# Splitting the memory copies of 41 segments into column halves, reordering the last scratch loads, and a new instruction order

## The chip, the cores and the metric

One core of a Trainium2 chip runs the whole program in a single launch. The metric is device time in microseconds (us), the median of three runs. Engine names are those of the profile: PE is TensorE (PEld its weight loads), DVE is VectorE, ACT is ScalarE, POOL is GpSimd, SP is the sync engine that issues most transfers.

## The reference

Two kinds of block alternate, A, B, A, B, each added to its own input `x` of 2048 tokens by 512 features. Block A is attention over 64 segments of 32 tokens with 8 memory rows in front, and the memory rows of a segment's output are the memory of the next segment:

```python
mem = mem0
for s in range(n_seg):                       # 64 segments, one after the other
    h = concatenate([mem, xs], axis=1)       # 8 memory rows + 32 tokens
    q, k, v = h @ Wq, h @ Wk, h @ Wv         # 512 -> 32 heads x 128
    p = softmax(where(mask, q @ k.T * scale, -1e9))
    o = (p @ v) @ Wo                         # 32 heads x 128 -> 512
    mem = o[:, :M, :]                        # carried to the next segment
    outs.append(o[:, M:, :])
```

Block B is linear attention over all tokens with `phi(t) = where(t > 0, t + 1, exp(t)) + 1e-6`; its sums over the sequence must be complete before its first output row:

```python
kv = sum over tokens of phi(k) outer v;  z = sum over tokens of phi(k)
o = (phi(q) @ kv) / (phi(q) @ z + 1e-6)
return o @ wo
```

So 128 segments (64 in each of two A blocks) form one serial chain through the memory rows, and the program's end is a block B that has to wait for the last segment.

## The kernel before

The code records operations (nodes) with the engines that may run them, what they read and write and the PSUM bank they use; nothing runs when they are recorded. Two tables written out by hand then decide the order. `PLACE` gives every node, under the key (layer, step, name) and its running number, a place in the order and, where two engines could do it, the letter of the engine (`a` ACT, `v` DVE); `BANKS` gives each PSUM tile one of eight banks. `schedule` sorts all nodes by the table and `finalize` turns dependences between engines into semaphore waits. Each engine runs its own list strictly in order, so a node that waits holds back everything behind it on that engine.

A segment is a step `s`. The names in `PLACE` that matter here:

- `kq0`, `kq1`, `v`: the projections of a segment's 40 rows by Wk, Wq and Wv (`project`). The contraction of 512 is done in four chunks `c` of 128, and `hT` holds the rows transposed, chunk by chunk. `kq0` does K and Q together, for each chunk four matmuls of Wk and four of Wq that share the stationary rows.
- `mem0`, `mem1`: scores, softmax and values of the memory queries, the part the next segment waits for.
- `out`: the output projection by Wo (`out_proj`), 64 matmuls of 256 columns into one PSUM tile. One copy then moves the tile (128 partitions x 256) to `outW`. Column halves 0:128 and 128:256 of `outW` hold what becomes chunks 0 and 2, and chunks 1 and 3, of the next segment's memory columns.
- `next` (`next_mem`): small matmuls with a selection matrix `selm`, four per half, transpose and add the memory rows into a PSUM tile of 32 columns; one copy writes them into the memory columns of `hT`. `kq0` of the next segment waits for that copy.
- `x`: the attention of the 32 tokens, which nothing waits for at once. It and the projections of other blocks (`left`, `bi`, `lq`, `bo`) fill PE while the chain above waits.

At the end, block B of the second layer (`last_rows`, `last_queries`, `b_out`) reads its inputs back from scratch memory in HBM, into the room of the A weights. SP loads, each after the one before it: `pt_scratch` (ready queries) into Wq's room, `xn_scratch` (normalized rows, whose queries are still to be computed) into Wk's room, and `xs_scratch` (the residual rows). `LATE[1]` names the eight row tiles 4 to 11 whose queries `last_queries` computes at the end, as PE work `lq` from `XN(4)` and `XN(8)`:

```python
for w, (vw, nm, free, t0) in enumerate(((pt_view, "pt", [], 3.4), (xs_view, "xs", rows, 3.4))):
    for i in range(0, NT - 1, 4):
        ...
        if prev is not None:
            nd.order.add(prev)
```

For i = 4 and 8 the first pass loads `xn_scratch`, for i = 0 and 12 `pt_scratch`. The load into Wk's room waits for the last matmul that reads Wk.

Of the kernel before, what the change touches and what calls it, by code (L numbers as in the profile page):

```python
# [1626 lines left out]
def c_dve(n, rate=1):  # L1627
    return 0.155 + 1.044e-3 * n / rate
# [246 lines left out]
def _build_kernel(nc, A_x, A_mem0, A_Wq, A_Wk, A_Wv, A_Wo, A_seg_len, B_wqkv, B_wo, out):  # L1875
# [3 lines left out]
    DH = A_Wq.shape[2]  # L1879
# [3 lines left out]
    NT = S // 128  # L1883
# [1184 lines left out]
```

## Time and profile before

| what | value |
|---|---|
| time, three runs | 1455.92, 1456.2, 1457.59 us; median 1456.2 |
| profiled execution | 1458.68 us, of which the span of the instructions is 1456.7 us |
| PE busy | 1432.7 us, 98% of the span, 43649 matmuls |
| DVE, ACT, POOL busy | 1241.8 (85%), 903.4 (62%), 202.5 us (14%) |
| mean granted TensorE clock | 0.999 |

PE's row says how much time is left to win: 1456.7 less 1432.7 is 24.0 us in which no matmul was under way. Matmuls overlap and their ends are modelled, so a wait of PE that is shorter than the last matmul's tail doesn't show as idle time; the weight-load queue's waits (PEld) show such short ones.

### The profile page before, as it was taken

To read this page: it belongs to the slowest core of one execution; us is meant where nothing else is said; L and a number is where in the kernel's file an instruction comes from. 1 tells how busy PE (TensorE), PEld (TensorE's weight loads), DVE (VectorE), ACT (ScalarE), POOL (GpSimd) and SP (SyncE) were. 2 spreads that over 40 slices of the span, in tenths; PEclk is the share of its full clock that TensorE was granted. 3 is DMA by queue.
4 is the path that set the end of the run, shared out by engine and by line. 5 is a ranking of instruction groups with operands and counts; after the bars stand their busy time and mean duration, and the time that the engine had idled before them with its cause. 6 is when DMAs were issued, how large, how long until landed. Compare 5 with 4: busy or idle time off the path is not lost.

```text
span 1456.7 us, 90916 instructions
## 1 busy us (share of the span) xinstructions
PE 1432.7 (98%) x43649; PEld 834.5 (57%) x39545; DVE 1241.8 (85%) x3910; ACT 903.4 (62%) x2588; POOL 202.5 (14%) x407
## 2 busy tenths in 40 slices
PE   9999999999999999999999999999999999999988
PEld 4555555555565656555465555565656655556555
DVE  6879888898888888888888888888888888888878
ACT  4456656556655666656656666666666666665547
POOL 3111111111111110111101111011101011111100
PEclk9999999999999999999999999999999999999999
DMA  9422112111110010101201111111101011110133
GB/s 384 177 60 39 33 28 47 25 25 25 23 25 22 14 26 24 26 25 49 75 16 22 36 32 26 28 29 36 25 18 25 26 28 29 25 26 21 35 76 128
DMA packets 79255, 66.96 MB, mean 46 GB/s; under 512 B 55480, under 2 KB 70648, under 8 KB 77336
## 3 DMA queue, kind: packets, MB, share of 16 engines
q1 hardware_dynamic: 64872, 42.04, 10.7%
q0 software_dynamic: 13840, 18.98, 4.5%
q8 instruction: 325, 5.32, 1.6%
q14 instruction: 58, 0.48, 0.1%
q10 hardware_dynamic: 160, 0.14, 0.0%
HBM read 31.33 MB, written 14.94 MB: 32 GB/s over the span
## 4 chain that ended last, share of the span: by engine, by line
PE 95%; DVE 2%; DMA 1%; ACT 1%; issue 1%; SPq 0%
PE pb L2283 44%; PE pb L2564 20%; PE pb L2140 15%; PE pb L2152 3%; PE pb L2514 3%; PE pb L2757 2%; PE pb L2472 2%; PE pb L2534 2%; PE pb L2436 2%; PE pb L2594 1%; DMA Wk_sb<-in_A_Wk_dram 1%; PE pb L2444 1%; DMA Wk_sb<-xn_scratch 1%; ACT arena_sb L2009 0%; DVE arena_sb L2489 0%
## 5 line engine op out<-in xcount | busy, mean ns | idle before, releaser
L2009 ACT ACTIVATE arena_sb<-pb 128x512 bf16<-128x512 f32 (+3 forms) x993 | 491.0, 524 | 240.6 <-PE pb L2140 112.0
L2283 PE MATMUL pb<-Wk_sb,arena_sb 128*32 128x512 bf16 x4320 | 358.7, 380 | 2.1 <-DVE arena_sb L2010 0.9
L2564 PE MATMUL pb<-Wo_sb,arena_sb 128*32 128x256 bf16 x10368 | 326.5, 273 | 1.4 <-issue 0.7
L2283 PE MATMUL pb<-Wv_sb,arena_sb 128*32 128x512 bf16 x4608 | 327.6, 378 | 0.0
L2564 PEld LDWEIGHTS pb<-Wo_sb,arena_sb 128*32 128x32 bf16 x10368 | 265.0, 97 | 43.9 <-DVE arena_sb L2479 12.9
L2302 DVE STREAM_TRANSPOSE arena_sb<-arena_sb 128x256 f32<-128x256 f32 x640 | 259.2, 426 | 27.1 <-ACT arena_sb L2009 20.1
L2027 POOL DMA_DIRECT2D dx_sb<-y_sb x246 | 125.0, 512 | 908.8 <-DVE y_sb L2576 398.0
L2283 PE MATMUL pb<-Wq_sb,arena_sb 128*32 128x512 bf16 x3088 | 234.4, 379 | 0.6 <-issue 0.6
L2283 PEld LDWEIGHTS pb<-Wk_sb,arena_sb 128*32 128x32 bf16 x4320 | 118.8, 96 | 177.6 <-issue 89.1
L2487 ACT ACTIVATE arena_sb<-pb,arena_sb 128x128 bf16<-128x128 f32 x538 | 163.8, 369 | 65.9 <-DVE arena_sb L2521 25.7
L2140 PE MATMUL pb<-Wq_sb,arena_sb 128*32 128x512 bf16 x2032 | 200.9, 379 | 0.0
L2010 DVE CAST arena_sb<-pb 128x512 bf16<-128x512 f32 (+2 forms) x274 | 141.9, 521 | 51.0 <-PE pb L2140 19.9
L2489 DVE TENSOR_TENSOR arena_sb<-pb,arena_sb 128x128 bf16<-128x128 f32 (+2 forms) x391 | 157.4, 403 | 8.6
L2009 ACT ACTIVATE outW_sb<-pb 128x256 f32<-128x256 f32 (+1 forms) x142 | 54.3, 383 | 174.5 <-PE pb L2564 124.4
L2283 PEld LDWEIGHTS pb<-Wv_sb,arena_sb 128*32 128x32 bf16 x4608 | 113.8, 95 | 70.6 <-issue 6.6
L2283 PEld LDWEIGHTS pb<-Wq_sb,arena_sb 128*32 128x32 bf16 x3088 | 85.1, 97 | 88.0 <-issue 25.2
L2514 PE MATMUL pb<-arena_sb 128*32 128x130 bf16 x3072 | 105.7, 219 | 1.1 <-issue 1.1
L2502 DVE TENSOR_TENSOR arena_sb<-arena_sb,wx_sb 128x1280 bf16<-128x1280 bf16 x128 | 102.2, 799 | 1.9 <-ACT arena_sb L2455 1.4
L2524 DVE STREAM_TRANSPOSE arena_sb<-arena_sb 128x192 f32<-128x192 f32 x256 | 93.4, 365 | 10.7 <-ACT arena_sb L2487 7.7
L2576 DVE TENSOR_TENSOR y_sb<-pb,outW_sb 64x256 bf16<-64x256 f32 x162 | 68.8, 424 | 19.8 <-ACT outW_sb L2009 15.3
L2514 PEld LDWEIGHTS pb<-arena_sb 128*32 128x32 bf16 x3072 | 67.3, 96 | 29.8 <-issue 8.5
L2472 PEld LDWEIGHTS pb<-arena_sb 128*32 128x32 bf16 x2016 | 47.3, 95 | 63.9 <-ACT arena_sb L2009 31.3
(135 smaller groups left out, 1819.1 us busy)
## 6 DMA issues: line engine op xcount, KB each, us to landing
Wk_sb<-in_A_Wk_dram SPq DMA_DIRECT2D x4, 1024.0 KB, 9.8
Wq_sb<-in_A_Wq_dram SPq DMA_DIRECT2D x4, 1024.0 KB, 17.7
Wv_sb<-in_A_Wv_dram SPq DMA_DIRECT2D x4, 1024.0 KB, 25.5
Wo_sb<-in_A_Wo_dram SPq DMA_DIRECT2D x8, 512.0 KB, 22.2
xs_scratch<-x_sb POOLq DMA_DIRECT2D x32, 128.0 KB, 2.0
pq_scratch<-arena_sb POOLq DMA_DIRECT2D x23, 128.0 KB, 2.1
xn_scratch<-arena_sb POOLq DMA_DIRECT2D x20, 128.0 KB, 2.9
lk_scratch<-arena_sb POOLq DMA_DIRECT2D x8, 256.0 KB, 3.5
```

The source lines that it names most:

```text
L2009: return e.activation(o() if callable(o) else o, i() if callable(i) else i, ACTF.Copy)
L2010: return e.tensor_copy(o() if callable(o) else o, i() if callable(i) else i)
L2027: add(eng, lambda e: e.dma_start(o, i), 0.55 if eng == "pool" else 0.66, reads=reads, writes=writes, dsem="%s%d" % (kind, k), lat=lat + (0 ...
L2140: return pe.add_instruction(mybir.InstMatmult(name=nc.get_next_instruction_name(), engine=mybir.EngineType.PE, ins=[pe.lower_ap(x), pe.low ...
L2283: r = pe.matmul(o, blk[:, c, :], w, start=(c == 0), stop=(c == 3), tile_position=(0, 32 * j))
L2302: add("dve", lambda v: v.transpose(dst, src(img[:, k, :].bitcast(F32))), 0.445, reads=[("img", k, h) for h in range(2)], writes=[dkey])
L2487: x = e.activation(o[:, u, :], i()[:, u, :], ACTF.Copy, scale=r[:, u:u + 1])
L2489: return e.tensor_tensor(o, i(), r.unsqueeze(2).to_broadcast([128, n, 128]), ALU.mult)
L2502: add("dve", lambda v: v.tensor_tensor(Px.rearrange("p b (n j x) -> p b n j x", n=20, j=4), PQx[:, r2].rearrange("p b (n x) -> p b n x", n ...
L2514: r = pe.matmul(pv.f32()[32 * i:32 * i + 32, 130 * k:130 * k + 130], cols(b, k, i), vimg[:, r2, 4 * b + i, :], start=True, stop=True, skip ...
L2524: add("dve", lambda v, b=b, k0=k0: v.transpose(oTb[:, s1, b, :, :, k0:k0 + 3].rearrange("p h j k q e -> p k (h j) (q e)").bitcast(F32), ox ...
L2564: r = pe.matmul(tl.f32()[32 * j:32 * j + 32, 0:256], oT[:, b, f, n, :, :, e], Wo_sb[:, 16 * b + 4 * n + 2 * f + e, 256 * d:256 * d + 256], ...
```

## The change

Three things are changed, and then everything is ordered anew.

1. `halved(s)` is true for steps 0 to 27 and 58 to 62 of the first layer and 0 to 2 and 58 to 62 of the second: 41 segments. In these the copy to `outW` is recorded as two copies of 128 columns; each half of `next` goes to a PSUM tile of its own and has its own copy, of 16 columns; and `kq0` of the segment that follows takes the chunks in the order 0, 2, 1, 3, of which 0 and 2 wait for the copy of half 0 and 1 and 3 for that of half 1.
2. The loads at the end go in the order i = 4, 8, 0, 12 in both passes: `xn_scratch` ahead of `pt_scratch`, and of the residual rows tiles 4 and 8 ahead of 0 and 12.
3. `PLACE` and `BANKS` are replaced as a whole.

```diff
+        def halved(s):
+            return (layer == 0 and (s < 28 or 57 < s < 63)) or (layer == 1 and (s < 3 or 57 < s < 63))
...
-            for c in range(4):
+            cs = (0, 2, 1, 3) if own else (0, 1, 2, 3)
+            for n, c in enumerate(cs):
...
-                add("pe", mm, 0.2155 * len(parts), reads=sorted({p[1] for p in parts}) + sorted({(p[1], 0, c) for p in parts}) + bkeys, tiles=tls)
+                add("pe", mm, 0.2155 * len(parts), reads=sorted({p[1] for p in parts}) + sorted({(p[1], 0, c) for p in parts}) + bkeys + (own[c % 2:c % 2 + 1] if own else []), tiles=tls)
...
-            nd = evac(outW[cc, v, :], lambda: tl.f32()[cc, 0:256], 256, tiles=[tl], writes=[("outW", w)])
-            nd.quad = (0, 0) if urgent else (2, 2)
+            c0 = P.count
+            for h in ((0, 1), (1, 2)) if urgent and halved(int(P.place[1])) else ((0, 2),):
+                if h[1] - h[0] < 2:
+                    P.count = 21 + h[0]
+                o = slice(128 * h[0], 128 * h[1])
+                evac(outW[cc, v, o], lambda o=o: tl.f32()[cc, o], 128 * (h[1] - h[0]), tiles=[tl], writes=[("outW", w, i) for i in range(*h)])
...
-                add("pe", mm, 0.06, reads=[("outW", w), "selm"], tiles=[tl])
+                add("pe", mm, 0.06, reads=[("outW", w, h), "selm"], tiles=[tls[h * apart]])
...
+            for h in range(2):
+                P.count = 11 + h
+                evac(dst[:, h], lambda h=h: tls[h].f32()[:, 16 * h:16 * h + 16].rearrange("p (d m) -> p d m", d=2), 16, tiles=[tls[h]],
+                     writes=[("hTm", G1 % 2, g1, h)])
...
-                    tk, tq = project(blk, bk, *parts)
+                    tk, tq = project(blk, bk[:1], *parts, own=bm) if s and halved(s - 1) else project(blk, bk, *parts)
...
-            for i in range(0, NT - 1, 4):
+            for i in (4, 8, 0, 12):
...
-    (0, 5, "next"): "96577 96655 96996v",
+    (0, 5, "next"): "95860 96108 0 0 0 0 0 0 0 0 0 96200a 96697v",
```

Where the tables put things is seen in the engines' lists. First PE, from the output projection of segment 5 of the first layer (`Wo_sb` x64) to the projections of segment 6 (`Wk_sb`, `Wq_sb`); `selm_sb,outW_sb` is `next`, 32x130 is token attention. Before:

```order
L2564 MATMUL pb<-Wo_sb,arena_sb 32x256 x64
L2514 MATMUL pb<-arena_sb 32x130 x24
L2534 MATMUL pb<-arena_sb 32x130 x8
L2594 MATMUL pb<-selm_sb,outW_sb 32x16 x8
L2283 MATMUL pb<-Wv_sb,arena_sb 32x512 x4
L2140 MATMUL pb<-Wv_sb,arena_sb 32x512 x4
L2283 MATMUL pb<-Wk_sb,arena_sb 32x512 x4
```

And now:

```order
L2569 MATMUL pb<-Wo_sb,arena_sb 32x256 x64
L2288 MATMUL pb<-Wv_sb,arena_sb 32x512 x4
L2140 MATMUL pb<-Wv_sb,arena_sb 32x512 x4
L2605 MATMUL pb<-selm_sb,outW_sb 32x16 x4
L2519 MATMUL pb<-arena_sb 32x130 x12
L2605 MATMUL pb<-selm_sb,outW_sb 32x16 x4
L2519 MATMUL pb<-arena_sb 32x130 x12
L2288 MATMUL pb<-Wk_sb,arena_sb 32x512 x4
```

The eight small matmuls of `next` stand apart as four and four, and the filling work around them has changed sides: the left block's Wv projection went ahead of `next`, the token attention behind it.

On ACT and DVE one copy to `outW` has become two, and one copy of `next` two; in 36 of the 41 segments both halves of the output copy stand one right after the other on ACT.

SP near the program's end, with the loads into the rooms of Wq and Wk. Before:

```order
L2027 DMA dx_sb<-y_sb 24x256 x2
L2933 DMA Wq_sb<-pt_scratch 128x4x512
L2925 DMA Wk_sb<-xn_scratch 128x4x512 x2
L2027 DMA dx_sb<-y_sb 24x256
L2181 DMA_TRANSPOSE arena_sb<-pq_scratch 128x4x128
L2027 DMA pt_scratch<-arena_sb 128x512
L2933 DMA Wq_sb<-pt_scratch 128x3x512
L2932 DMA Wq_sb<-xs_scratch 128x4x512 x3
L2932 DMA Wq_sb<-xs_scratch 128x3x512
```

And now:

```order
L2027 DMA dx_sb<-y_sb 24x256 x2
L2943 DMA Wk_sb<-xn_scratch 128x4x512 x2
L2181 DMA_TRANSPOSE arena_sb<-pq_scratch 128x4x128
L2027 DMA dx_sb<-y_sb 24x256
L2951 DMA Wq_sb<-pt_scratch 128x4x512
L2027 DMA pt_scratch<-arena_sb 128x512
L2951 DMA Wq_sb<-pt_scratch 128x3x512
L2950 DMA Wq_sb<-xs_scratch 128x4x512 x3
L2950 DMA Wq_sb<-xs_scratch 128x3x512
```

The first load of ready queries went behind the two loads of rows, a transpose and a small move.

PE at the same end, from the last matmuls that read Wk as a weight to the first that compute queries from the loaded rows (`Wk_sb,arena_sb` under L2152). Before:

```order
L2283 MATMUL pb<-Wk_sb,arena_sb 32x512 x4
L2283 MATMUL pb<-Wv_sb,arena_sb 32x512 x4
L2564 MATMUL pb<-Wo_sb,arena_sb 32x256 x48
...
L2283 MATMUL pb<-Wv_sb,arena_sb 32x512 x24
L2564 MATMUL pb<-Wo_sb,arena_sb 32x256 x8
L2514 MATMUL pb<-arena_sb 32x130 x12
L2564 MATMUL pb<-Wo_sb,arena_sb 32x256 x16
L2514 MATMUL pb<-arena_sb 32x130 x12
L2534 MATMUL pb<-arena_sb 32x130 x16
L2564 MATMUL pb<-Wo_sb,arena_sb 32x256 x40
L2152 MATMUL pb<-Wk_sb,arena_sb 32x512 x16
```

And now:

```order
L2288 MATMUL pb<-Wk_sb,arena_sb 32x512 x16
L2569 MATMUL pb<-Wo_sb,arena_sb 32x256 x8
L2288 MATMUL pb<-Wq_sb,arena_sb 32x512 x8
L2288 MATMUL pb<-Wv_sb,arena_sb 32x512 x8
L2288 MATMUL pb<-Wq_sb,arena_sb 32x512 x8
L2569 MATMUL pb<-Wo_sb,arena_sb 32x256 x16
...
L2569 MATMUL pb<-Wo_sb,arena_sb 32x256 x40
...
L2288 MATMUL pb<-Wv_sb,arena_sb 32x512 x24
L2569 MATMUL pb<-Wo_sb,arena_sb 32x256 x8
L2519 MATMUL pb<-arena_sb 32x130 x12
L2539 MATMUL pb<-arena_sb 32x130 x8
L2152 MATMUL pb<-Wk_sb,arena_sb 32x512 x8
```

Left out in both are the scores' small matmuls, and before also 4 of Wv. Between the last use of Wk and the first use of the loaded rows there stood 32 matmuls by Wv, 112 by Wo and 40 of 130 columns; now there stand 32 by Wv, 16 by Wq, 72 by Wo and 20 of 130 columns.

More of the change, by code (lines that the diff above doesn't have):

```diff
@@ new lines @@
+    "6251745023450346220532345024026251353560426305243205340605273146743670671437630437304637704564035645"
+    "4171024103654127504374073076074245563436635217462764422521406624154752024060504757714605120465341062"
+    "3451274317362417337627436274716235714736146236561014471036540132710327074203154623724505607423754235"
+    "3042735405074372071560075436072153647534601731543672037210102473204703406516360532502365201460503465"
+    "2103570245246730264571025015213524713716505742034012543561435214305701556312304027107026130752043623"
@@ new lines @@
+    "2464676754024736042363512647325667106431006521716430567707236102734027746027703245561406541265164751"
+    "0745700461570515754602167242427366254702432410377023012150321604245366424236253524700536143204623471"
+    "2173551274513243461253070614763647516520135621256026013101442357601740510152731603612062560203476445"
+    "1674205747560247301524125725031641725637452472540075260471671363613063010751276414726047604261054741"
+    "0146441075216506130536340537065072560523720723607730760451670516041567300740411536207457250714105724"
@@ new lines @@
+    "0572475012632361437652746516274412564752652113624260452163571270275174205352407015047510707145165475"
+    "7011537366132327041534540560314357761060714363571423605370213174021357647056014462651357310463104135"
+    "0410627561732061756737664230751067407365073623072102041535144720647216020261367504235640635240205013"
+    "1647520767274062754267755742164513305476260744241565731246071524136020367205612345713741527305724317"
+    "1625065461310774330272036440157243167540301563126750432675456732560451466405320127170512360344320465"
@@ L1604 @@
+    "0626536245335312476507360473137562035165203452740760274506120115072167135053740231420142061275302725"
+    "6307211561546530120744376423241736070474072321054140760746276025307406310234510651067435275067142647"
+    "1627415076647420734033613205717250672046527014751204653015721072746503214571032470157463276327463263"
+    "1275467236325140150306452473541060070574417727643303025272221"
 )
@@ L2260, in at, with project, mm @@
             P.at(layer, s, name)
-        def project(blk, bkeys, *parts, fresh=0):
+        def halved(s):
+            return (layer == 0 and (s < 28 or 57 < s < 63)) or (layer == 1 and (s < 3 or 57 < s < 63))
+        def project(blk, bkeys, *parts, fresh=0, own=None):
             tls = [P.tile() for _ in parts]
-            for c in range(4):
-                def mm(pe, c=c):
+            cs = (0, 2, 1, 3) if own else (0, 1, 2, 3)
+            for n, c in enumerate(cs):
+                def mm(pe, c=c, n=n):
+                    first, last = n == 0, n == 3
                     for i, (tl, (W, key, b, across, *lo)) in enumerate(zip(tls, parts)):
@@ L2277, in mm @@
                             else:
-                                n = (8 * j + 4 * b) * DH
-                                w = W[:, c, n + lo:n + hi]
+                                at_ = (8 * j + 4 * b) * DH
+                                w = W[:, c, at_ + lo:at_ + hi]
                             if i and 4 * c + j >= fresh:
-                                r = again(pe, o, blk[:, c, :], w, c == 0, c == 3, (0, 32 * j))
+                                r = again(pe, o, blk[:, c, :], w, first, last, (0, 32 * j))
                             else:
-                                r = pe.matmul(o, blk[:, c, :], w, start=(c == 0), stop=(c == 3), tile_position=(0, 32 * j))
+                                r = pe.matmul(o, blk[:, c, :], w, start=first, stop=last, tile_position=(0, 32 * j))
                     return r
-                add("pe", mm, 0.2155 * len(parts), reads=sorted({p[1] for p in parts}) + sorted({(p[1], 0, c) for p in parts}) + bkeys, tiles=tls)
+                add("pe", mm, 0.2155 * len(parts), reads=sorted({p[1] for p in parts}) + sorted({(p[1], 0, c) for p in parts}) + bkeys + (own[c % 2:c % 2 + 1] if own else []), tiles=tls)
             return tls
@@ L2588, in next_mem, with mm @@
             G1, g1 = divmod(s + 1, 4)
-            tl = P.tile()
+            apart = halved(s)
+            tls = [P.tile() for _ in range(1 + apart)]
             for h in range(2):
-                def mm(pe, h=h):
+                def mm(pe, h=h, tl=tls[h * apart]):
                     for j in range(4):
@@ L2596, in mm @@
                     return r
-                add("pe", mm, 0.06, reads=[("outW", w), "selm"], tiles=[tl])
-            evac(hT[:, G1 % 2, g1, :, 0:8].rearrange("p (d h) m -> p h d m", d=2),
-                 lambda: tl.f32()[:, 0:32].rearrange("p (h d m) -> p h d m", h=2, d=2), 32, tiles=[tl],
-                 writes=[("hTm", G1 % 2, g1)])
+                add("pe", mm, 0.06, reads=[("outW", w, h), "selm"], tiles=[tls[h * apart]])
+            dst = hT[:, G1 % 2, g1, :, 0:8].rearrange("p (d h) m -> p h d m", d=2)
+            if not apart:
+                evac(dst, lambda: tls[0].f32()[:, 0:32].rearrange("p (h d m) -> p h d m", h=2, d=2), 32, tiles=tls,
+                     writes=[("hTm", G1 % 2, g1, h) for h in range(2)])
+                return
+            for h in range(2):
+                P.count = 11 + h
+                evac(dst[:, h], lambda h=h: tls[h].f32()[:, 16 * h:16 * h + 16].rearrange("p (d m) -> p d m", d=2), 16, tiles=[tls[h]],
+                     writes=[("hTm", G1 % 2, g1, h)])
         def rows_out(k, G, moves):
@@ L2672, in a_layer @@
         at(-4, "start")
[L2673 removed]
+        evac(hT[:, 0, 0, :, 0:8], memT0_sb[:, :, :], 32, reads=["memT0"], writes=[("hTm", 0, 0, 0), ("hTm", 0, 0, 1)])
         ty = tokens(0, -6)
@@ L2689, in a_layer @@
             blk = hT[:, G % 2, g, :, :]
-            bk = [("hTm", G % 2, g), ("hTx", G % 2, g)]
+            bm = [("hTm", G % 2, g, h) for h in range(2)]
+            bk = [("hTx", G % 2, g)] + bm
             if g == 0 and G + 1 < NT and not (first and G < 2):
```

35 lines of the change are left out of this document (8 added, 27 removed), and 3114 rows, old and new, of the table PLACE.

## The prediction

> **What bounds the kernel now.** The page comes first, and says that PE is the bound: it is busy for all but 24 us. Time can only be won from those 24 us, or lost by adding to them.
>
> ```profile
> span 1456.7 us, 90916 instructions
> PE 1432.7 (98%) x43649; PEld 834.5 (57%) x39545; DVE 1241.8 (85%) x3910; ACT 903.4 (62%) x2588; POOL 202.5 (14%) x407
> ```
>
> The busy time by stretches then says where they lie. Columns: stretch, its length, busy time and instructions of PE, PEld, DVE, ACT and POOL, the granted TensorE clock, DMA share, GB/s. The stretches hold, in this order, the halved segments 1 to 27 of the first layer, its segments 58 to 62, the change of layers with segments 0 to 2 of the second, the segments between, 58 to 62 of the second, and three pieces of the end.
>
> ```profile
> 48.00:320.00 272.00, 266.79 (x8300) 155.11 (x7604) 237.01 (x771) 161.49 (x469) 39.53 (x77) 1.00 0.19 45
> 610.00:670.00 60.00, 59.40 (x1864) 34.68 (x1700) 48.60 (x160) 35.52 (x103) 8.47 (x17) 1.00 0.09 23
> 670.00:735.00 65.00, 62.30 (x1764) 34.09 (x1616) 56.08 (x165) 39.88 (x104) 11.29 (x24) 1.00 0.24 66
> 735.00:1355.00 620.00, 617.67 (x19056) 364.72 (x17152) 536.47 (x1705) 398.51 (x1170) 81.93 (x158) 1.00 0.12 28
> 1355.00:1411.00 56.00, 55.33 (x1760) 32.98 (x1584) 47.90 (x152) 31.06 (x85) 6.74 (x13) 1.00 0.14 40
> 1411.00:1415.00 4.00, 0.98 (x36) 0.69 (x28) 2.02 (x6) 1.00 (x3) 0.00 (x0) 1.00 0.88 173
> 1415.00:1420.00 5.00, 4.61 (x88) 3.22 (x92) 1.91 (x4) 0.69 (x2) 0.00 (x0) 0.66 0.13 34
> ```
>
> PE is idle for 5.2 us in the early halved segments, 0.6, 2.7 and 0.7 in the other three stretches that hold some, and only 2.3 us in the 620 us between, where nothing can be won. At the end 3.0 of 4 us are lost at once, and the next 5 us run at a clock of 0.66.
>
> The timelines of PE and SP around 1411 us name that loss (start, length, engine, line, operation, count; in brackets the idle time and what ended it).
>
> ```profile
> 1406.08 0.39 PE L2283 MATMUL pb<-Wv_sb,arena_sb 128*32 128x512 bf16 x4
> 1410.70 1.27 PE L2564 MATMUL pb<-Wo_sb,arena_sb 128*32 128x256 bf16 x40
> 1415.39 1.72 PE L2152 MATMUL pb<-Wk_sb,arena_sb 128*32 128x512 bf16 x16 [3.42 <-DMA Wk_sb<-xn_scratch]
> 1429.89 1.82 PE L2152 MATMUL pb<-Wq_sb,arena_sb 128*32 128x128 bf16 x110
> 1433.05 0.23 PE L2152 MATMUL pb<-Wq_sb,arena_sb 128*32 128x128 bf16 x2 [1.34 <-issue]
> 1406.08 0.39 SPq L2933 DMA_DIRECT2D Wq_sb<-pt_scratch  x1
> 1406.52 1.48 SPq L2925 DMA_DIRECT2D Wk_sb<-xn_scratch  x2
> 1419.24 2.27 SPq L2932 DMA_DIRECT2D Wq_sb<-xs_scratch  x4
> ```
>
> PE has nothing to do from 1411.97 until the second load of rows lands, which was issued behind the load of ready queries that PE first touches at 1429.89.
>
> The chain between segments is read from the timeline of one early segment, PE, ACT and DVE together.
>
> ```profile
> 57.28 0.38 ACT L2009 ACTIVATE outW_sb<-pb 128x256 f32<-128x256 f32 x1 [1.46 <-PE pb L2564]
> 57.72 0.32 PE L2594 MATMUL pb<-selm_sb,outW_sb 128*32 128x16 f32 x16
> 58.13 0.19 DVE L2010 CAST arena_sb<-pb 128x32 bf16<-128x32 f32 x1 [0.28 <-PE pb L2594]
> 58.38 0.40 PE L2283 MATMUL pb<-Wk_sb,arena_sb 128*32 128x512 bf16 x4 [0.34 <-DVE arena_sb L2010]
> 58.82 0.39 PE L2283 MATMUL pb<-Wk_sb,arena_sb 128*32 128x512 bf16 x4
> ```
>
> Each link starts some 0.06 us after the one before has ended: copy, `next`, copy, projection. PE ran out of filling work and stood for 0.34 us. How often, the weight-load queue's waits tell (total us, times, longest), first for 48 to 320 us, then for 610 to 670, 670 to 735 and 1355 to 1411; only waits on the memory chain are shown.
>
> ```profile
> PEld pb L2283 <- DVE arena_sb L2010: 4.7, 15, 0.5
> PEld pb L2594 <- ACT outW_sb L2009: 4.4, 13, 0.7
> PEld pb L2283 <- ACT arena_sb L2009: 1.6, 5, 0.4
> ...
> PEld pb L2283 <- DVE arena_sb L2010: 0.7, 2, 0.4
> ...
> PEld pb L2283 <- ACT arena_sb L2009: 1.1, 4, 0.3
> ...
> PEld pb L2283 <- ACT arena_sb L2009: 0.6, 2, 0.3
> ```
>
> **The end, part by part.** The loads' times to landing come from the table of transfers (count, size, median us from issue to landing).
>
> ```profile
> Wk_sb<-xn_scratch SPq DMA_DIRECT2D x2, 512.0 KB, 6.7
> Wq_sb<-pt_scratch SPq DMA_DIRECT2D x1, 512.0 KB, 3.7
> ...
> Wq_sb<-xs_scratch SPq DMA_DIRECT2D x3, 512.0 KB, 6.1
> Wq_sb<-xs_scratch SPq DMA_DIRECT2D x1, 384.0 KB, 8.7
> ```
>
> The three loads share one path: the first lands after 3.7 us, at 1409.8. The third, issued at about 1407.5, lands at 1415.39, after 7.9. The two loads of rows have the middle value 6.7, so the second took about 5.5 and landed at 1412.0, 5.9 us after the first was issued. With the rows first, the load that PE waits for goes from third to second. Its release does not change: the first load of rows was issued 0.44 us after 1406.08, when PE left Wk. So the rows land at 0.44 + 5.9, some 6.4 us after that point, and not at 9.3.
>
> When does PE want them? Before, its work from there lasted 1411.97 - 1406.08 = 5.9 us. By the order, 40 matmuls of 256 columns and 20 of 130 go from this stretch and 16 of 512 come. Eight of 512 take 58.82 - 58.38 = 0.44 us, 0.055 each, and the others in proportion 0.028 and 0.014: 5.9 - 1.1 - 0.3 + 0.9 = 5.4 us. A stall of 6.4 - 5.4 = 1.0 us stays, and 2.4 of the 3.4 go. Bounds: nothing stays, or 2.7, if the load that PE waits for takes the middle value 6.7 from an issue 1.0 us behind the first (0.44 + 1.0 + 6.7 - 5.4).
>
> The slow clock after the stall costs (1 - 0.66) x 5 = 1.7 us. The pause of 1.34 us before 1433.05 is as long as the one that stays. From 1420 on the clock is back:
>
> ```profile
> 1420.00:1457.00 37.00, 31.10 (x840) 19.08 (x832) 31.12 (x63) 27.48 (x52) 0.55 (x1) 0.99 0.39 126
> ```
>
> So a pause of that length didn't bring the clock down here, and I take the 1.7 us as won. The Trainium skill's page "TensorE: Matmul & The Clock Gate" (Part 1, "What's actually happening") says the clock falls after an idle window of about 3.4 us that runs free of the kernel. By that rule a stall of 3.42 us meets such a window in some executions only, and in those without it the sum below would be 1.7 us smaller; the trace shows one execution and can't tell.
>
> What is late next: the residual rows. Tile group 0 went from first to third of the four, and PE now needs it with the first output rows. Before, these rows stood at 1429.89, 14.5 us after the first query matmul, 12.8 without the slow clock; now 112 - 72 = 40 Wo matmuls that were ahead of it come between, 1.1 us. That is 6.4 + 12.8 + 1.1 = 20.3 us after PE left Wk. SP began the four issues 13.2 us after that point, about 0.55 each; the third lands 6.1 to 8.7 us after its own, at 20.4 to 23.0. A new wait of 0 to 2.7 us; I take 0.7, nearer the lower end: the transpose that stands ahead of them on SP waits for a store that shared the path with three loads and now shares it with two, so SP should come to them sooner. The queries' load itself, now behind a transpose, has over 15 us of cover; without that cover it would cost its 3.7 us. The transposes, small moves and the store to `pt_scratch` only change places among transfers that PE doesn't wait for in this stretch. End: 2.4 + 1.7 - 0.7 = 3.4 us won.
>
> **The halved segments, part by part.** Three rows give the prices of the copies.
>
> ```profile
> L2009 ACT ACTIVATE outW_sb<-pb 128x256 f32<-128x256 f32 x120 | 46.0, 383 | 164.1 <-PE pb L2564 121.9 <-PE pb L2514 39.7 <-PE pb L2835 2.2
> L2009 ACT ACTIVATE arena_sb<-pb 128x32 bf16<-128x32 f32 x57 | 11.2, 196 | 23.2 <-PE pb L2514 12.3 <-PE pb L2594 8.1 <-PE pb L2534 1.0
> 1408.11 0.53 ACT L2455 ACTIVATE arena_sb<-pb 128x160 bf16<-128x160 f32 x2
> ```
>
> 383 ns for 256 columns and 196 for 32 give, on a straight line, 276 for 128: the first half is there 0.11 us sooner. `next` on it is half as long, 0.03 us less, and the copy of 16 columns costs no less than 0.19. So the projection can start 0.14 us sooner. The second half follows on ACT at about 0.2 us (two copies of 160 columns take 0.53), and ends 0.1 us later than the whole copy did; its chunks stand behind two chunks of K and Q, 2 x 0.44 us of PE work, which hide it. The sum into `y` waits for both halves, but goes to a store with segments of time.
>
> Each wait of a projection on the memory copy is worth 0.14 us at most; they number 20 early and 2, 4 and 2 in the other stretches. 28 x 0.14 = 3.9 us; some are waits of other segments' projections in these stretches, and 3.5 is what I take. Bounds: nothing, or all 41 segments, 5.7 us, about the 5.2 + 0.6 + 0.7 of idle time that there is. The new order elsewhere moves matmuls whose number is the same, through stretches with 2.3 us of idle time: taken at nothing, between 1 us won and 2 lost.
>
> **The sum.** 3.4 + 3.5 = 6.9 us, from the profiled execution's 1458.7 to 1451.8. That execution stands 2.5 us above the median of the runs, and the slow clock may be part of why. Half of the 1.7 us is therefore not counted against the median: 1456.2 - 6.9 + 0.85 gives 1450.2 us.
>
> **The rivals.** *The copies' halves bring nothing.* The waits move to the next link of the chain, since PE lacks filling work there too (0.34 us of idle time in the segment shown). Then only the end is won, 3.4 us and in a run without the slow clock 1.7: 1452.8 to 1454.5. For it speaks that scores and values wait in the same segments, against it that the filling work set free can be put there.
>
> *Everything is won.* No stall stays at the end, 5.1 us, and the chain gives its 5.7: 1445.4. Against it speaks the residual rows' place.
>
> *Slower: the extra copies get in the way on ACT and DVE.* Each halved segment adds 0.13 us of output copies (0.28 + 0.23 against 0.38) and a copy of 0.19, 0.32 in all, on engines that run in order, and DVE is busy for 237.01 of 272 us there. If those copies stand ahead of what PE waits for next (images of K and Q, transposes), the segment loses 0.32 - 0.14 = 0.18 us, 41 x 0.18 = 7.4, and with the end's 3.4 won the run takes 4.0 us more: 1460.2. It decides where ACT and DVE have less than 0.32 us to spare between the memory copy and the first copy of the projections; by the rows that gap holds four chunks, 4 x 0.44 us. The Trainium skill's page "VectorE: DVE Perf Modes" ("The TRN2 errata") gives ScalarE reading PSUM a fixed 172 cycles per instruction, which speaks against splitting: by it two halves cost an estimated 500 ns where one copy costs 357, again 0.14 us more; the measured 383 lies a little above.
>
> **How the numbers follow.** The forecast has 0.58, the rival without gain from the halves 0.20, everything won 0.10, slower 0.12. This measurement can tell about 0.2%, 2.9 us, from no change, so 1453.3 and below is faster: forecast and full gain, and half of the first rival, 0.78. The other half is 0.10 for the same, and 0.12 slower. The range reaches from near the full gain, 1446.5, to 1454.8, just past the first rival's upper end; it leaves out the slower case and the extremes.
>
> **What would show it.** Right: PE's wait at the rows' load falls to about 1 us with the clock at 1.00 behind it; PE's idle time from 48 to 320 us falls from 5.2 to about 3; the wait of `next` on the output copy becomes shorter. Wrong: a wait of PE for `xs_scratch` over 1 us, waits of scores and values that grow by as much as those of the projections shrink, or ACT and DVE waits where the added copies stand.

## The result, and the profile after

The changed kernel takes 1452.31 us (median of 9 runs, 1451.26 to 1453.33), the kernel before 1457.02 us (9 runs on the same chip, 1454.89 to 1459.9). The ratio is 0.9966, 95% interval 0.9956 to 0.9977: faster, by 4.7 us of the median. The forecast was 1450.2 us, with 1446.5 to 1454.8 as its range.

The profiled execution took 1452.79 us. The head of its page, and its busy time by stretches (length, then PE, PEld, DVE, ACT, POOL, granted clock, DMA share, GB/s):

```profile
span 1450.1 us, 90972 instructions
PE 1429.3 (99%) x43649; PEld 840.4 (58%) x39545; DVE 1249.2 (86%) x3938; ACT 897.9 (62%) x2600; POOL 203.4 (14%) x407
```

```profile
48.00:320.00 272.00, 267.51 (x8340) 161.00 (x7636) 240.33 (x783) 164.14 (x513) 39.30 (x76) 1.00 0.18 45
...
735.00:1355.00 620.00, 618.34 (x19112) 364.63 (x17200) 539.48 (x1716) 393.29 (x1141) 81.97 (x159) 1.00 0.12 27
...
1410.00:1415.00 5.00, 5.00 (x168) 4.07 (x172) 3.47 (x10) 1.84 (x5) 0.00 (x0) 1.00 0.45 143
1415.00:1420.00 5.00, 4.67 (x124) 2.15 (x116) 4.26 (x11) 3.21 (x8) 0.52 (x1) 1.00 0.83 284
```

PE's idle time from 48 to 320 us went from 5.2 to 4.5 us only; behind the end's stall the clock stays at 1.00. The timeline of PE at the end, where PE leaves Wk (the row ahead of 1403.47), where it first wants the loaded rows, and where the first output rows begin:

```profile
1403.47 0.41 PE L2569 MATMUL pb<-Wo_sb,arena_sb 128*32 128x256 bf16 x8
...
1408.47 0.29 PE L2539 MATMUL pb<-arena_sb 128*32 128x130 bf16 x8
1409.97 0.61 PE L2152 MATMUL pb<-Wk_sb,arena_sb 128*32 128x512 bf16 x8 [1.20 <-DMA Wk_sb<-xn_scratch]
...
1424.79 0.85 PE L2152 MATMUL pb<-Wq_sb,arena_sb 128*32 128x128 bf16 x48 [0.53 <-DVE arena_sb L2911]
```

The stall is 1.20 us, and the wait ahead of the output rows is for DVE, not for residual rows. The weight-load queue's waits from 48 to 320 us, on the memory chain:

```profile
PEld pb L2288 <- ACT arena_sb L2009: 4.6, 12, 1.0
...
PEld pb L2605 <- ACT outW_sb L2009: 3.2, 8, 0.6
PEld pb L2288 <- DVE arena_sb L2010: 2.9, 9, 0.6
...
PEld pb L2605 <- DVE outW_sb L2010: 0.5, 2, 0.3
```

Before, `next` waited for copies on DVE too, beside the 4.4 us for ACT that the prediction shows:

```profile
PEld pb L2594 <- DVE outW_sb L2010: 0.4, 2, 0.2
```

So the waits of `next` fell from 4.8 us in 15 to 3.7 in 10, but those of the projections grew from 6.3 us in 20 to 7.5 in 21. Yet the chain itself is shorter. The same early segment, ACT, DVE and PE:

```profile
58.52 0.28 ACT L2009 ACTIVATE outW_sb<-pb 128x128 f32<-128x128 f32 x1 [1.32 <-PE pb L2519]
...
58.85 0.26 PE L2605 MATMUL pb<-selm_sb,outW_sb 128*32 128x16 f32 x8
...
58.91 0.26 DVE L2010 COPY outW_sb<-pb 128x128 f32<-128x128 f32 x1
58.93 0.24 PE L2519 MATMUL pb<-arena_sb 128*32 128x130 bf16 x4
...
59.17 0.17 DVE L2010 CAST arena_sb<-pb 128x16 bf16<-128x16 f32 x1
...
59.23 0.26 PE L2605 MATMUL pb<-selm_sb,outW_sb 128*32 128x16 f32 x8
...
59.40 0.40 PE L2288 MATMUL pb<-Wk_sb,arena_sb 128*32 128x512 bf16 x4
```

From the first output copy to the first projection it is 59.40 - 58.52 = 0.88 us; before it was 58.38 - 57.28 = 1.10. Between the two parts of `next` stands other PE work, as in 31 of the 41 halved segments. That the second half is copied on another engine than the first is not typical: it is so in 4 of the 41.

### The profile page after: what moved, and what is told of

Same layout as the page of the kernel before. It is cut to its first block, busy times and chain, and to the rows that moved or that the text cites. A ratio compares the mean times of both kernels' runs of the same rounds, so it can differ in the third digit from the quotient of the medians.

```text
span 1450.1 us, 90972 instructions
## 1 busy us (share of the span) xinstructions
PE 1429.3 (99%) x43649; PEld 840.4 (58%) x39545; DVE 1249.2 (86%) x3938; ACT 897.9 (62%) x2600; POOL 203.4 (14%) x407
## 3 DMA queue, kind: packets, MB, share of 16 engines
q8 instruction: 325, 5.32, 1.5%
## 4 chain that ended last, share of the span: by engine, by line
PE 92%; DVE 5%; DMA 1%; issue 1%; ACT 1%; POOL 0%; POOLq 0%
PE pb L2288 43%; PE pb L2569 19%; PE pb L2140 14%; PE pb L2519 3%; PE pb L2775 2%; PE pb L2477 2%; PE pb L2539 2%; PE pb L2441 2%; PE pb L2152 1%; PE pb L2605 1%; DVE arena_sb L2010 1%; DVE Wq_sb L3013 1%; PE pb L2449 1%; DMA Wk_sb<-xn_scratch 0%; DVE arena_sb L2494 0%
## 5 line engine op out<-in xcount | busy, mean ns | idle before, releaser
L2009 ACT ACTIVATE arena_sb<-pb 128x512 bf16<-128x512 f32 (+4 forms) x1038 | 503.1, 512 | 258.4 <-PE pb L2140 119.1
L2494 DVE TENSOR_TENSOR arena_sb<-pb,arena_sb 128x128 bf16<-128x128 f32 (+2 forms) x420 | 171.2, 408 | 9.3
L2492 ACT ACTIVATE arena_sb<-pb,arena_sb 128x128 bf16<-128x128 f32 x467 | 142.9, 369 | 56.4 <-DVE arena_sb L2546 17.6
L2009 ACT ACTIVATE outW_sb<-pb 128x256 f32<-128x256 f32 (+2 forms) x177 | 56.0, 337 | 164.4 <-PE pb L2569 122.7
L2010 DVE CAST arena_sb<-pb 128x512 bf16<-128x512 f32 (+3 forms) x265 | 134.5, 511 | 25.9 <-PE pb L2140 9.6
```

The lines of the kernel that those rows point to most:

```text
L2009: return e.activation(o() if callable(o) else o, i() if callable(i) else i, ACTF.Copy)
L2010: return e.tensor_copy(o() if callable(o) else o, i() if callable(i) else i)
L2492: x = e.activation(o[:, u, :], i()[:, u, :], ACTF.Copy, scale=r[:, u:u + 1])
L2494: return e.tensor_tensor(o, i(), r.unsqueeze(2).to_broadcast([128, n, 128]), ALU.mult)
```

## The experiments

Times are medians; each ratio is to the kernel before, run in turn on the same chip (there 1457.26, 1457.03 or 1457.04 us).

**Both kernels once more.**

> The changed kernel once more, beside the three that follow, so that they are compared on one chip. If the differences between the two traces at the program's start (the first `next` comes 1.3 us later than before the change) and at the end (a stall of 1.2 us, granted clock 1.00 behind it) belong to the order, this profile shows them again, within 0.3 us; if they are chance, the start moves by about a microsecond. Time: 1452.3 us, 4 to 5 below the kernel before.

> The kernel before, so that the granted clock of each of its runs is on record. If the slow clock behind the stall of 3.4 us comes in every execution, the mean clock of each run is 0.999 and they agree; if it comes only in some, the runs fall into two groups, 0.999 and 1.000, about 1.7 us apart (by the first trace: 5 us at 0.66). Time: 1457 us.

The changed kernel took 1451.98 us (ratio 0.9970, 0.9958 to 0.9981), with a stall of 1.40 us, clock 1.00, and the first `next` at 49.27 us: start and end are the order's own. The kernel before took 1456.72 us, but its second profile has another end:

```profile
1413.83 1.05 PE L2152 MATMUL pb<-Wk_sb,arena_sb 128*32 128x512 bf16 x16 [1.28 <-DMA Wk_sb<-xn_scratch]
```

```profile
1415.00:1420.00 5.00, 5.00 (x144) 3.49 (x137) 3.61 (x9) 1.75 (x5) 0.00 (x0) 1.00 0.25 65
```

The stall was 1.28 us where the first profile had 3.42, with the clock at 1.00 and not 0.66. So the profile behind the prediction showed a bad case of something that varies.

How often the clock falls is told by the mean granted clock of each run. It is 0.999 or 0.998 in 32 of 75 runs of the kernel before, on three chips, and 1.000 in the others. On each chip the runs with the lower clock have the longer spans in the mean, by 0.8, 1.2 and 2.3 us, but the two groups overlap and aren't set 1.7 us apart as was expected. Of the 15 runs of the changed kernel none has the lower clock; of all 66 runs in the new order, those of the experiments below included, 2 have it; of the 31 experiment runs in the old order 18, among them 5 of 12 with the loads' order alone. So the full clock at the end comes with the new order, not with the loads' order by itself.

With the starts of `next` (L2594 before, L2605 now) as marks, two profiles of each kernel give:

| piece | before | now | won, by the means |
|---|---|---|---|
| start to the first `next` | 47.98, 48.12 | 49.29, 49.27 | -1.2 |
| 27 early halved segments | 272.96, 272.34 | 271.83, 271.35 | 1.1 |
| next 30 segments | 314.56, 315.13 | 314.16, 314.18 | 0.7 |
| 5 segments, halved (58 to 62) | 51.78, 52.35 | 52.28, 52.28 | -0.2 |
| change of layers, 3 halved | 75.67, 75.61 | 75.45, 75.00 | 0.4 |
| 54 segments | 585.43, 585.57 | 584.12, 585.62 | 0.6 |
| 5 segments, halved | 53.14, 52.98 | 52.92, 53.11 | 0.0 |
| last `next` to the end | 55.20, 51.05 | 50.02, 50.25 | 3.0 |

The sum is 4.4 us. The end's 3.0 us rest on two profiles of before that differ by over 4 us there; against the second alone 0.9 are won.

**The halves undone.** In the changed kernel's order:

```diff
-            for h in ((0, 1), (1, 2)) if urgent and halved(int(P.place[1])) else ((0, 2),):
+            for h in ((0, 2),):            # place and engine of the first half
...
-                add("pe", mm, 0.06, reads=[("outW", w, h), "selm"], tiles=[tls[h * apart]])
+                P.count = 0 if apart else P.count; add("pe", mm, 0.06, reads=[("outW", w, h), "selm"], tiles=[tls[0]])
...
-            if not apart:
+            if True:                       # one copy of 32 columns
```

> The changed kernel with whole copies: in all halved segments one copy of 256 columns of the output and one of 32 behind `next`, at the place and on the engine of the first half, the two parts of `next` next to each other; all other instructions in the changed kernel's order. Forecast's theory: the separate halves are worth 3.5 us, so this kernel takes about 1455.8. From the two traces (the 27 early halved segments together take 1.1 us less than before): 1453.5. Rival (the waits only move to the next link): within 0.5 us of the changed kernel, 1452.3; it would be faster than that if the extra copies cost more than the waits bring.

1455.29 us, 3.3 above the changed kernel on the same chip (ratio 0.9988, 0.9979 to 0.9997, against 0.9970). The forecast's 3.5 us hold. In the same segment the chain is back at 59.90 - 58.80 = 1.10:

```profile
58.80 0.39 ACT L2009 ACTIVATE outW_sb<-pb 128x256 f32<-128x256 f32 x1 [1.32 <-PE pb L2519]
...
59.24 0.32 PE L2605 MATMUL pb<-selm_sb,outW_sb 128*32 128x16 f32 x16
...
59.65 0.19 DVE L2010 CAST arena_sb<-pb 128x32 bf16<-128x32 f32 x1 [0.17 <-PE pb L2519]
59.90 0.40 PE L2288 MATMUL pb<-Wk_sb,arena_sb 128*32 128x512 bf16 x4 [0.28 <-DVE arena_sb L2010]
```

But by its one profile the 27 early segments take 273.45 us, 0.8 more than the mean of the kernel before, which has whole copies too, and the four halved stretches together 1.5 more. In these stretches the new order without the halves is the worse one.

**Half copies, waits joined.** Instructions that would stand ahead of what they now wait for are put right behind it.

```diff
-                add("pe", mm, 0.06, reads=[("outW", w, h), "selm"], ...
+                P.count = 1 if apart else P.count; add("pe", mm, 0.06, reads=[("outW", w, 0), ("outW", w, 1), "selm"], ...
...
-                    tk, tq = project(blk, bk[:1], *parts, own=bm) if s and halved(s - 1) ...
+                    tk, tq = project(blk, bk, *parts, own=bm) if s and halved(s - 1) ...
```

> The changed kernel with all its half copies, but without separate waits: both parts of `next` wait for both halves of the output, and the projection's first chunk for both halves of the memory copy; otherwise the same order. The difference to the changed kernel is what the separate waits bring, the difference to the kernel with whole copies is what the extra copies cost. Forecast's theory: separate waits bring 0.14 us in 28 waits, so 1456, and the extra copies cost nothing, so the same as with whole copies. Rival (other work fills the time): 1452.5 to 1453. Rival of the extra copies in the way on ACT and DVE: over 2 us slower than the kernel with whole copies.

1468.63 us (ratio 1.0084, 1.0071 to 1.0097): 16.7 above the changed kernel and 13.3 above whole copies. That is past the last rival's bound of 2 us, but the extra copies as such aren't the reason: the changed kernel has the same ones.

```profile
58.36 0.28 ACT L2009 ACTIVATE outW_sb<-pb 128x128 f32<-128x128 f32 x1 [1.32 <-PE pb L2519]
...
58.75 0.26 DVE L2010 COPY outW_sb<-pb 128x128 f32<-128x128 f32 x1
59.06 0.32 PE L2605 MATMUL pb<-selm_sb,outW_sb 128*32 128x16 f32 x16 [0.19 <-DVE outW_sb L2010]
...
59.48 0.18 ACT L2009 ACTIVATE arena_sb<-pb 128x16 bf16<-128x16 f32 x1 [0.84 <-PE pb L2605]
59.72 0.40 PE L2288 MATMUL pb<-Wk_sb,arena_sb 128*32 128x512 bf16 x4 [0.33 <-ACT arena_sb L2009]
```

The second half's copy starts 0.39 us behind the first, and all the chain now stands behind it: 59.72 - 58.36 = 1.36. Worked out in this way for 26 early segments, the mean from the first output copy to the projection is 1.22 and 1.20 us in the two profiles of before, 1.18 with the halves undone, 1.07 and 1.03 in the changed kernel, and 1.46 here. 41 x (1.46 - 1.05) = 16.8 us, near the 16.7 of the runs; by the marks of the table above the halved stretches take 14.3 us more than in the changed kernel. So here nearly all that the chain loses is lost in time.

**The halves alone, in the old order.** The changed code with the old table, the copies' halves at the place of the whole ones:

```diff
-                    P.count = 21 + h[0]
+                    P.count = c0           # both halves at the old copy's place
...
-            tls = [P.tile() for _ in range(1 + apart)]
+            tls = [P.tile()] + [_Tile(banks, None)] * apart   # a bank that is free there
```

> The kernel before with the half copies alone: in the halved segments two output copies, two parts of `next` with a wait each, two memory copies and chunks 0, 2, 1, 3, each at the old place of the whole one and on its engine, the two parts of `next` next to each other in PE's order, the second memory copy's bank picked among those free; order of all else and of the loads as before. Forecast's theory: 28 waits x 0.14 us, 3.5 us less, 1453.7. Rival: other work fills the time, no change, 1457.2. Rival with the other sign: in this order the second part of `next` stands right behind the first and waits for the second half, which is there 0.1 us later than the whole copy was; the first projection stands behind it on PE, so 0.1 us in each of 28 waits are lost, 1460.

1462.75 us (ratio 1.0041, 1.0027 to 1.0055): 5.7 slower, near the rival with the other sign. The chain's mean is 1.36, or 41 x 0.15 = 6.2 us. But the waits of `next` from 48 to 330 us name a part that the edit itself brought, the earlier user of the bank picked for the second part:

```profile
PEld pb L2605 <- DVE y_sb L2586: 1.1, 3, 0.4
...
PEld pb L2605 <- ACT arena_sb L2492: 0.8, 2, 0.5
PEld pb L2605 <- DVE arena_sb L2761: 0.8, 2, 0.6
```

That is 2.7 us. So the loss is shown; how much of it is the halves' own is open.

A round from one segment to the next is the chain and the rest, from the first projection to the next segment's first output copy. Their means over the 27 early rounds, in us, from the profiles:

| kernel | chain | rest |
|---|---|---|
| before, two profiles | 1.21, 1.20 | 8.90, 8.89 |
| changed, two profiles | 1.06, 1.03 | 9.00, 9.02 |
| halves undone | 1.17 | 8.96 |
| waits joined | 1.45 | 8.95 |
| halves alone, old order | 1.35 | 8.87 |

Against the kernel before the chain is 0.16 us shorter in the changed one and the rest 0.12 longer, so only about a quarter of the chain's gain reaches the time. About half of the longer rest is there with whole copies too, so it belongs to the new order.

**The loads' order alone, in the old order.**

```diff
-            for i in range(0, NT - 1, 4):
+            for i in (4, 8, 0, 12):         # and the table's times of these loads exchanged
```

> The kernel before with the new order of its last loads alone (rows ahead of queries, groups 4, 8, 0, 12), all else in its old order. Forecast's theory: the second load of rows lands 6.4 us after PE leaves Wk, and PE's other work there lasts 5.9 us, so the stall falls from 3.4 to 0.5 us and the slow clock behind it goes; the residual rows take back 0 to 1 us: 3 to 4.5 us below the kernel before, 1452.5 to 1454.5. Rival (the residual rows or the queries' load become the wait): less than 1.5 us, over 1455.5.

1457.70 us (ratio 1.0003, 0.9993 to 1.0014): nothing is won. The theory's first half came true, the second did not. PE's timeline:

```profile
1411.64 1.05 PE L2152 MATMUL pb<-Wk_sb,arena_sb 128*32 128x512 bf16 x16
1412.52 0.50 PE L2564 MATMUL pb<-Wo_sb,arena_sb 128*32 128x256 bf16 x10
1415.03 0.73 PE L2564 MATMUL pb<-Wo_sb,arena_sb 128*32 128x256 bf16 x20 [2.01 <-issue]
```

The rows are there in time, and 26 matmuls on, within a run of equal ones and with no semaphore to wait for, PE stands for 2.01 us. The transfers by queue (packets, MB, share of 16 engines), first from 1406.6 to 1412.6 and then to 1413.8 us, and the clock behind:

```profile
q1 hardware_dynamic: 1599, 1.57, 78.8%
...
q8 instruction: 1, 0.02, 5.4%
```

```profile
1415.00:1420.00 5.00, 4.97 (x100) 4.50 (x103) 2.42 (x6) 0.38 (x1) 0.00 (x0) 0.66 0.15 45
```

While the three loads fill the path no instruction packet comes; one of 16384 bytes comes at 1412.71, and PE goes on 1.3 us behind its end. In nearly all profiles PE's long pauses of this kind near the end stand at the same matmuls, whatever the order: behind the 42754th or 42755th, 384 on, and 128 on from there (the exceptions: one of 0.96 us 128 ahead of the second place, two of 0.81 and 0.27 us at the 42084th, and in the run with the waits joined two that come seven matmuls earlier). The Trainium skill's page "Runtime: NRT & Kernel Launch" ("Instruction fetch mechanics") says that an engine's program is streamed in blocks of 16 KiB, 256 instructions, which the packet's size bears out (128 matmuls with their weight loads are 256); it calls the cost "mostly hidden", and here it isn't. In the first profile of before this block came at 1413.10, inside the stall for the rows: two waits with one end, of which the forecast saw one.

**The ready queries' load later, and sooner.** First the kernel with the loads alone, that load behind the next transpose; then the changed kernel, that load right behind the rows:

```diff
-    (1, 64, "ldpq"): "1402452",
+    (1, 64, "ldpq"): "1407000",
```

```diff
-    (1, 64, "ldpq"): "1402232",
+    (1, 64, "ldpq"): "1397459",
```

> The kernel before with its last loads of rows first, as in the run with the loads alone, and the load of the ready queries moved further back, behind the transpose that follows (where the changed kernel has it). In the run with the loads alone the second rows landed at 1411.60, but PE then stood for 2.01 us at its matmul 42755; a block of 16384 bytes on the instruction queue was moved at 1412.71 to 1413.75, while three loads of 512 KB were under way until 1413.46, and PE went on 1.3 us behind it. Theory (PE waits for its program, which stands behind the loads): with one load of 512 KB less the block comes some 1.5 us sooner, the pause falls to 0.5 us or less, the clock stays at 1.00: 2 to 3.5 us faster than the loads alone, 1454 to 1455.5. Rival (the pause belongs to the rows' loads themselves or to PE): the pause stays near 2 us, 1457.5.

> The changed kernel with the load of the ready queries moved forward, right behind the two loads of rows; no instruction of PE, ACT, DVE or POOL moves. Theory (program blocks stand behind the loads): the block that PE needs at its matmul 42754 comes 1 to 2 us later than 1409.7, and a pause of 0.5 to 1.5 us appears there, 0.5 to 1.5 us slower than the changed kernel: 1452.8 to 1453.8. Rival (no link): no pause at 42754, 1452.2.

Later: 1457.58 us (ratio 0.9998, 0.9988 to 1.0008), no gain, though the pause at that block shrank as expected. It came back at a later block, with the slow clock behind it:

```profile
1416.13 1.71 PE L2564 MATMUL pb<-Wo_sb,arena_sb 128*32 128x256 bf16 x54 [0.34 <-issue]
```

```profile
1432.48 0.23 PE L2152 MATMUL pb<-Wq_sb,arena_sb 128*32 128x128 bf16 x2 [2.80 <-issue]
```

```profile
1432.50:1437.50 5.00, 5.00 (x158) 3.84 (x161) 4.33 (x7) 2.31 (x5) 0.00 (x0) 0.66 0.02 3
```

Sooner: 1454.0 us (ratio 0.9974, 0.9965 to 0.9983), 1.7 to 2.0 above the changed kernel's two medians and a little past the range expected, with no instruction of PE moved. The block comes at 1411.82 instead of 1409.68, its pause appears, and the rows come 0.7 us later too:

```profile
1410.66 0.61 PE L2152 MATMUL pb<-Wk_sb,arena_sb 128*32 128x512 bf16 x8 [1.89 <-DMA Wk_sb<-xn_scratch]
...
1414.38 1.71 PE L2569 MATMUL pb<-Wo_sb,arena_sb 128*32 128x256 bf16 x55 [0.51 <-issue]
```

So the loads hold the program back, in both orders. In the changed kernel 101 matmuls, not 26, stand between the rows' first use and that block; that this is why its end gains where the loads alone gain nothing fits all these rows, but was not tried by itself. Nor was the new order with the loads in their old order, so how much of the end's gain the loads bring there is open.

**Rows 8 first, and the start mended.** The stall that is left ends with the second of the two loads:

```diff
-            for i in (4, 8, 0, 12):
+            for i in (8, 4, 0, 12):
```

> The changed kernel with the loads in the order 8, 4, 0, 12 in place of 4, 8, 0, 12. If the 1.2 us that PE still waits end with the second load of rows and the first one landed 1.5 us earlier (1408.44 against 1409.92, PE's demand at 1408.77), the stall goes: 1451.1, with PE's first touch of the other rows at 0.5 us behind, where they land at about 1410: up to 0.7 us of it may come back there. Rival: what PE does first behind the stall is bound elsewhere (the residual rows, the copies on DVE), so 1452.3 as before.

1450.60 us (ratio 0.9960, 0.9946 to 0.9973), 1.4 below the changed kernel on the same chip; in the profile PE doesn't wait for the rows.

```profile
1406.65 0.29 PE L2539 MATMUL pb<-arena_sb 128*32 128x130 bf16 x8
1406.77 0.60 PE L2152 MATMUL pb<-Wk_sb,arena_sb 128*32 128x512 bf16 x8
...
1410.36 1.71 PE L2569 MATMUL pb<-Wo_sb,arena_sb 128*32 128x256 bf16 x55 [0.24 <-issue]
```

At the start of the changed kernel the third transpose stands behind 16 matmuls, with nothing ahead of its copies' end; before, it stood ahead of such matmuls:

```profile
13.56 0.40 PE L2208 MATMUL pb<-id_sb,arena_sb 128*32 128x128 bf16 x16
14.96 1.26 PE L2288 MATMUL pb<-Wk_sb,arena_sb 128*32 128x512 bf16 x20 [0.99 <-ACT arena_sb L2009]
```

```diff
-    (0, 2, "prep"): "... 12288 ...",      (0, 3, "sk"): "13652 ...
+    (0, 2, "prep"): "... 11424 ...",      (0, 3, "sk"): "13868 ...
```

(and the two moves on ACT and DVE that the expectation names)

> The changed kernel with the loads 8, 4, 0, 12 and two pieces of its first 15 us in another order: the third transpose of PE stands ahead of 16 matmuls on Wk instead of behind them (PE waited 0.99 us for the copies of its result), and on ACT and DVE the first rows' scale is no longer behind the second rows' (PE's wait of 0.94 us for it against 0.38 before the change). If these two places are what makes the first `next` come 1.3 us later than before the change, it comes at 48.0 again and the time is 1.2 us below that with the loads 8, 4, 0, 12 alone, about 1449.4. Rival: the start is bound by the weights' arrival, and `next` stays at 48.9: 1450.6.

> The changed kernel with the loads in the order 8, 4, 0, 12 once more, beside the next one on the same chip: 1450.6.

> The same with the mended first 15 us once more. In its first profile the first `next` came 0.93 us sooner than with the loads 8, 4, 0, 12 alone, and the 120th 1.05 us; the span was not shorter, since PE stood 0.57 and 0.97 us for program blocks at the end. If the start's gain comes through, 0.9 us below the kernel above, 1449.7; if the pauses at the end belong to this order, the same time, 1450.6.

With the start mended the first `next` comes at 47.97 and 48.19 us, and the last one 0.6 and 3.1 us sooner than in the profiles with rows 8 first alone. The time does not follow: 1450.96 and 1451.91 us (ratios 0.9953 and 0.9964), against 1450.60 and 1451.44 (0.9960 and 0.9962). From the last `next` to the end these profiles take 50.4 and 50.8 us, against 49.3 and 49.7: part of the gain is given back there, in larger pauses at the program's blocks. The two can't be told apart. Rows 8 first, with or without the mended start, is the best version shown, about 1 us below the changed kernel, with intervals that overlap its own.

## Why the prediction was right, and where it was not

**The end** was put at 3.4 us won, by the means 3.0 were. Its steps: PE wants the rows 5.4 us after it leaves Wk (measured 5.3: 1403.47 to 1408.76, the stall's start), they land at 6.4 (1409.97 - 1403.47 = 6.5), a stall of 1.0 stays (1.20 and 1.40). The 0.7 us for residual rows were not there: no wait for them. Two steps failed without harm to the sum. The stall of 3.42 us and the slow clock were taken for the kernel's state; the second profile has 1.28 and a full clock, and against that one the stall is no shorter now. Half of the clock's 1.7 us was kept out of the median, near the 32 of 75 runs that have it, but none of the stall; that 3.4 and 3.0 lie close is partly luck. And "what is late next" is not the residual rows but PE's own program: the loads alone win nothing, and the end was won only in the new order.

**The halves** were put at 3.5 us, and undoing them costs 3.3. That agreement is partly luck. The price of 0.14 us fits the chain, whose mean is 0.13 longer with the halves undone (1.18 against 1.05), but the gain is in the mean of all rounds and not in 28 waits: 41 x 0.13 = 5.3 us, of which 3.3 reach the time. And against the kernel before, the four halved stretches win only 1.1 - 0.2 + 0.4 + 0.0 = 1.3 us. The step that failed is the one that priced the halves in the old order and took "the new order elsewhere" at nothing beside them: in the early rounds the rest grew by 0.12 us where the chain fell by 0.16, and with whole copies the new order costs 1.5 us in the halved stretches. The sign that was named, PE's idle time from 48 to 320 us falling to about 3, didn't come: it is 4.5. In the runs the half copies paid only in the new order (the run in the old one has the bank's waits in it), where other PE work mostly stands between the two parts of `next`; what that work alone is worth was not tried.

**The rest at nothing**: -1.2 us at the start, which the forecast never looked at, and 1.3 in the long stretches between. That they cancel is luck, and the 1.3 are within what two profiles of one kernel differ by (584.12 and 585.62); the range of that term, 2 lost to 1 won, held the sum.

**The sum**: forecast were 3.4 + 3.5 - 0.85, some 6.0 us below the median. The pieces measured are 3.0 + 1.3 + 0.1 = 4.4, and the runs show 4.7 and 5.3. What is short is the halves' term, by 2.2 us. The time, 1452.31, is inside the range, but it lies 2.1 us above the forecast and only 0.5 below the first rival's 1452.8 to 1454.5 (whose lower end counts the clock's 1.7 us in full, where the forecast counts half).

**The rivals.** That the halves bring nothing fell with the run that undoes them. Its mechanism, waits that move to the next link, is there all the same: in the waits of the projections, and in the rest of the round, which takes back 0.12 of the 0.16 us. That the extra copies get in the way was not far off: the joined waits cost 16.7 us, and in the old order the halves lost. What decided with the waits joined is not the room on ACT and DVE, as the rival had it, but that the second half's copy stands in the chain.

## What to carry to other kernels

A stall that ends with a load may hide a second wait with the same end: before a load is moved, ask what the engine needs next, its own program included, and look at the transfers by queue. Splitting a copy shortens a serial chain only if the second half is off it, with a wait of its own; otherwise it adds its fixed cost to every round. What a shorter link is worth is read from the whole round, since the rest can take it back. And one profile of a stall on a crowded path is one draw: take a second before it goes into a sum.

## What the runs showed of the hardware

The program's blocks (325 packets on queue q8, 5.32 MB, so 16.4 KB each) share the path with the loads: with 512 KB loads under way PE stood up to 2.01 and 2.80 us for one, and went on 1.2 to 1.6 us behind the end of its packet.

The slow clock is 0.50 for 3.41 us, which makes the 0.66 over 5 us. In all 14 profiles the clock changes only on a grid of steps of 3.41 us, whose start differs from profile to profile. After it first reached 1.00 it fell behind every step in which PE was busy for 1.40 us or less, and behind none in which it was busy for 1.65 or more:

| kernel | step, us | PE busy in it, us | clock in the next step |
|---|---|---|---|
| before, first profile | 1412.21 to 1415.62 | 0.23 | 0.50 |
| queries later | 1429.55 to 1432.96 | 0.61 | 0.50 |
| loads alone | 1412.74 to 1416.15 | 1.40 | 0.50 |
| rows 8 first | 1442.86 to 1446.27 | 1.65 | 1.00 |
| queries sooner | 1406.95 to 1410.36 | 1.82 | 1.00 |
| halves alone | 1413.83 to 1417.25 | 2.40 | 1.00 |
| halves alone | 1417.25 to 1420.66 | 2.42 | 1.00 |

So the pause of 2.01 us with the loads alone, which lies within one step, brought the clock down, and the stall of 2.02 us with the halves alone did not: an edge of the grid cuts it into 1.03 and 0.99 us. The Trainium skill's page "TensorE: Matmul & The Clock Gate" (Part 1, "What's actually happening") has an idle window of about 3.4 us, free-running. The grid agrees; but a window needn't be wholly idle, since one with 1.40 us of work in it was enough here.
